# Half of the second layer's weight conversion moved behind the recurrence, as whole tiles in SBUF

## The chip, the cores and the metric

The kernel runs on one core of a Trainium2 chip. The metric is the device time of one execution in microseconds (us); the time of a kernel is the median of several executions. The engines are named as the profile names them: PE (TensorE matmuls), PEld (TensorE weight loads), DVE (VectorE), ACT (ScalarE), POOL (GpSimd) and SP (SyncE, which here issues nearly all DMAs). Each engine works through its own instructions in order, and waits for semaphores.

## The reference

A recurrence over 768 steps for 32 heads (batch 4, 8 heads, width 40) is followed by two feed-forward layers on 3072 tokens. All weights arrive as float64.

```
for t in range(S):                      # recurrence, per head
    y[t]  = r[t] @ state
    Sa    = state @ a[t]
    state = state * w[t] - outer(Sa, b[t]) + outer(v[t], k[t])
x = relu(y @ w_in) ** 2 @ w_out         # layer 0: 320 -> 2048 -> 320
h = x @ w_in2
out = (h * cos(h)) @ w_out2             # layer 1
```

## The kernel before

**The recurrence in chunks.** The 768 steps are cut into 12 chunks of 64, and one call of `period(c)` (line 1013) writes the instructions of one chunk as 42 ticks. At each tick a table `todo` calls generator steps: `decay`, `gt`, `state`, `merge` and their loads and stores. The order in which these Python calls are made is the order in which every engine meets its instructions; nothing is rearranged later. An engine that waits holds up everything behind it.

**The solver.** Each chunk needs a small triangular system solved: `solve` (line 442) issues 62 elementwise operations and a copy (line 454, `L<-T`). From chunk 2 on it runs on POOL, two or three operations per tick from tick 9 to tick 36. When the copy is done, `solve_store` (lines 461, 463) puts the result in DRAM, `load_t` (lines 470, 476) brings it back in another layout for `merge`, and `solve_load` (lines 434 to 439) brings the next system's `T`, `L` and `l21` in, at tick 6 of the next chunk. All these are DMAs of the SP queue. I call the time from one copy's end to the next a cycle: its front lasts until the next solver's first operation, the rest is its solve phase.

**The layers between.** `Mlp.pipeline` (line 772) is a generator over blocks of 512 tokens (6 per layer) and 16 tiles of 128 hidden units. Of one tile it issues 8 matmuls into `h` (line 839), then 8 into `po` (line 795, layer 0) or 12 into `pt` (line 785, layer 1) for the tile two earlier, and gives control back after every second matmul. In layer 0 a tile takes three ACT operations (lines 693 to 695) and one subtraction on POOL (`gl`, line 696). During the recurrence `period` takes about 1.5 such steps per tick; block 5 of layer 0 needs the last chunk, and so starts behind the recurrence, as does all of layer 1.

**The conversion of float64.** There is no float64 on the engines. `Weights` takes each number as two 32-bit words: `clamp` (two ACT operations, lines 167 and 168, and one on DVE), `bits` (two on DVE), `add` (one on POOL, line 179). `pieces` (line 248) does so by quarter tiles of 256, 128, 160 and 160 columns, one piece every 5 steps: at step 0 SP loads the words into `w` (line 183; 2 buffers), at step 4 comes the clamp, then bits and add, and at step 10 the end. For layer 1 (`second`, line 276) the end is a DMA that stores the float32 piece `u` (2 buffers) to the DRAM tensor `w2f` (line 278). So the clamp of piece k+2 must wait until the store of piece k has landed, and the load of piece k+2 until the add of piece k is done. From chunk 2 on, `period` advances the conversion by one step in each tick (line 1093): first the last four tiles of layer 0, then the 16 tiles of layer 1.

**Behind the recurrence.** A range check (`range_sum`; its matmul `pb` is at line 932) is issued, the recurrence's buffers are given up, and a pool `m3` is opened in their place. While the last block of layer 0 runs, `load_w2` (line 670) fetches each converted tile from `w2f` into `wr` (8 buffers), and `split_w2` (line 675) makes the weights' high and low parts of it two steps ahead of their use. A second program, `General`, stands behind a branch that is not taken with these inputs.

## Time and profile before

| what | value |
|---|---|
| median of 3 runs | 1291.02 us (1290.79 to 1295.07) |
| the profiled execution: time | 1293.38 us |
| its span, first to last instruction | 1291.6 us |
| PE busy in the span | 1075.1 us (83%) |
| DVE, ACT, POOL busy | 712.9 (55%), 702.4 (54%), 671.1 us (52%) |
| DMA moved | 121.74 MB, mean 94 GB/s |
| mean granted TensorE clock | 0.897 of full speed |

The stages have different limits. Until about 871 us the recurrence runs, with layer 0 threaded through it; from then on block 5 of layer 0 (to about 943 us) and layer 1 run alone, and PE hardly pauses. Busy shares over the whole span mix the two. In the rows below, a bracket at a row's end gives the time that the engine was idle before the instruction, and what ended that idle time.

### The profile page before, as it was taken

The numbers are of one execution on the slowest core, as the hardware profiler recorded it, in microseconds if no ns is written. First come the engines' busy times: TensorE is split into PE (matmuls) and PEld (weight loads), VectorE is DVE, ScalarE is ACT, GpSimd is POOL, SyncE is SP. The second block draws the span as 40 slices with busy tenths as digits, with TensorE's granted clock in tenths as the row PEclk, the third lists the DMA queues.
The fourth block names the chain that finished last, engine by engine and source line by source line (L and its number), as shares of the span: only waits on it lengthen the run. The fifth ranks groups of instructions, "written<-read, shape, count | busy, mean of one in ns | idle before, by whom it ended". The sixth has DMA issues, their size and how long they took to land.

```text
span 1291.6 us, 27044 instructions
## 1 busy us (share of the span) xinstructions
PE 1075.1 (83%) x10242; PEld 902.2 (70%) x10242; DVE 712.9 (55%) x1450; ACT 702.4 (54%) x1492; POOL 671.1 (52%) x1067
## 2 busy tenths in 40 slices
PE   3245636787879898969797899799999999999997
PEld 3144536666657676757676678578889999999996
DVE  6869765576656665736665546221197343444432
ACT  4133644566566566655656556556556565655554
POOL 4112585685739482838474747423586333333332
PEclk9985555788979898988898889899999999999998
DMA  6473744546373838373745454413031010101000
GB/s 178 83 170 92 174 113 97 115 94 137 71 182 93 171 82 190 93 156 84 159 128 119 113 131 114 88 41 134 19 117 41 5 46 1 46 1 45 1 21 24
DMA packets 281168, 121.74 MB, mean 94 GB/s; under 512 B 231013, under 2 KB 259173, under 8 KB 279885
## 3 DMA queue, kind: packets, MB, share of 16 engines
q1 hardware_dynamic: 279195, 119.24, 38.8%
q8 instruction: 83, 1.36, 0.4%
q10 hardware_dynamic: 1834, 0.69, 0.2%
q14 instruction: 56, 0.46, 0.1%
HBM read 91.31 MB, written 28.57 MB: 93 GB/s over the span
## 4 chain that ended last, share of the span: by engine, by line
PE 50%; POOL 16%; DMA 12%; DVE 10%; SPq 5%; issue 4%; ACT 3%; POOLq 0%; ACTq 0%; DVEq 0%
PE h L839 22%; PE pt L785 13%; PE po L795 7%; DMA cin<-cin 6%; POOL T L451 5%; POOL ttmp L448 4%; POOL gl L696 3%; DMA w2f<-u 2%; POOL u L179 2%; PE px L573 2%; DVE u L142 2%; DVE T L451 1%; DVE ttmp L448 1%; DVE cin L142 1%; PE pu L581 1%
## 5 line engine op out<-in xcount | busy, mean ns | idle before, releaser
L839 PE MATMUL h<-xh,ws 128*128 128x512 f32 x960 | 333.8, 411 | 22.5 <-ACT g L693 22.2
L839 PE MATMUL h<-xl,ws 128*128 128x512 f32 x576 | 235.5, 409 | 0.0
L839 PEld LDWEIGHTS h<-xh,ws 128*128 128x128 f32 x960 | 185.9, 195 | 66.2 <-ACT g L693 26.2
L724 POOL TENSOR_TENSOR gl<-g,gh 128x512 fp32r<-128x512 f32 x96 | 125.2, 1304 | 190.9 <-ACT gh L723 163.6
L179 POOL TENSOR_TENSOR u<-u,w 128x256 int32<-128x256 int32 (+2 forms) x104 | 75.4, 725 | 222.0 <-DVE u L142 142.3
L696 POOL TENSOR_TENSOR gl<-g,gh 128x512 fp32r<-128x512 f32 x96 | 126.7, 1320 | 116.8 <-ACT gh L695 108.9
L142 DVE TENSOR_SCALAR u<-u 128x256 f32<-128x256 f32 (+2 forms) x208 | 72.5, 349 | 172.9 <-ACT u L167 171.2
L795 PE MATMUL po<-gh,ws 128*128 128x512 f32 x480 | 142.8, 422 | 0.3 <-DVE o L142 0.3
L448 POOL TENSOR_TENSOR ttmp<-T,L 128x126 f32<-128x126 f32 (+22 forms) x310 | 124.9, 403 | 34.0 <-DMA L<-Ls 14.0
L451 POOL TENSOR_TENSOR T<-T,ttmp 128x126 f32<-128x126 f32 (+22 forms) x310 | 131.3, 424 | 19.3
L785 PE MATMUL pt<-ws,gh 128*128 128x320 f32 x768 | 128.1, 308 | 0.5 <-DVE g L142 0.4
L839 PEld LDWEIGHTS h<-xl,ws 128*128 128x128 f32 x576 | 112.5, 195 | 20.2
L785 PEld LDWEIGHTS pt<-ws,gh 128*128 128x128 f32 x768 | 119.9, 188 | 8.3 <-DVE g L142 0.6
L142 DVE SCALAR_TENSOR_TENSOR g<-n,h 128x512 f32<-128x512 int32 x96 | 66.0, 687 | 103.3 <-ACT n L704 100.4
L704 ACT ACTIVATE n<-h 128x512 int32<-128x512 f32 x96 | 57.3, 596 | 119.9 <-PE h L839 119.8
L693 ACT ACTIVATE g<-h 128x512 f32<-128x512 f32 x96 | 57.0, 594 | 109.8 <-PE h L839 109.2
L407 PE MATMUL pgt<-at,cin 40*128 40x104 f32 x768 | 72.1, 329 | 52.1 <-DVE at L142 21.4
L795 PEld LDWEIGHTS po<-gh,ws 128*128 128x128 f32 x480 | 94.0, 201 | 24.0 <-issue 1.7
L142 DVE TENSOR_TENSOR g<-g,h 128x512 f32<-128x512 f32 x96 | 65.8, 685 | 71.7 <-ACT g L708 71.7
L167 ACT ACTIVATE u<-w 128x256 f32<-128x256 f32 (+2 forms) x104 | 40.8, 392 | 117.9 <-DMA w2f<-u 73.7
L407 PEld LDWEIGHTS pgt<-at,cin 40*128 40x128 f32 x768 | 62.0, 230 | 59.1 <-issue 24.9
L795 PE MATMUL po<-gl,ws 128*128 128x512 f32 x288 | 85.5, 400 | 0.0
(100 smaller groups left out, 2308.5 us busy)
## 6 DMA issues: line engine op xcount, KB each, us to landing
rv<-rv SPq DMA_DIRECT2D x48, 256.0 KB
cin<-cin SPq DMA_DIRECT2D x11, 832.0 KB
w<-moe SPq DMA_DIRECT2D x12, 704.0 KB
w<-moe SPq DMA_DIRECT2D x40, 160.0 KB
Ls<-ga SPq DMA_DIRECT2D x48, 128.0 KB
L<-Ls SPq DMA_DIRECT2D x48, 128.0 KB
wr<-w2f SPq DMA_DIRECT2D x16, 352.0 KB
w<-moe SPq DMA_DIRECT2D x20, 256.0 KB
```

The costliest lines, as they stand in the source:

```text
L142: fn(*args, **kwargs)
L179: self.nc.gpsimd.tensor_tensor(t.bitcast(I32), u.bitcast(I32), w[:, :, 0], op=ALU.add)
L407: nc.tensor.matmul(pv[par][:, j], self.kb[r0:r0 + 40, p0 + j].rearrange("p h b -> p (h b)"), self.at[r0:r0 + 40, p0 + j], start=True, stop ...
L448: eng.tensor_tensor(tv, T[:, 0:r, j:j + 1].to_broadcast([128, r, n]), L[:, j:j + 1, j + 1:32].to_broadcast([128, r, n]), op=ALU.mult)
L451: eng.tensor_tensor(T[:, 0:r, j + 1:32], T[:, 0:r, j + 1:32], tv, op=ALU.add)
L693: nc.scalar.activation(g, h, AF.Relu)
L696: self.later.append((2, lambda: nc.gpsimd.tensor_tensor(gl, g, gh, op=ALU.subtract)))
L704: nc.scalar.activation(n, h, AF.Copy, bias=0.25, scale=float(np.float32(1.0 / (2.0 * np.pi))))
L724: nc.gpsimd.tensor_tensor(gl, g, gh, op=ALU.subtract)
L785: nc.tensor.matmul(self.pos[j][:, 0:DM], x[:, 128 * j:128 * j + 128], wo[:, DM * ws:DM * ws + DM], start=(f == 0 and x is gh and ws == 0), ...
L795: nc.tensor.matmul(self.pos[m], wo[:, 128 * ws:128 * ws + 128], x, start=(f == 0 and k in (0, 2, 4)), stop=(f == NF - 1 and k in (5, 6, 7)))
L839: nc.tensor.matmul(h, wi[:, ws], x[:, kt], start=(k == 0), stop=(k == 7))
```

## The change

`LATE = 8`: `second` now converts only tiles 0 to 7 of layer 1 in pieces during the recurrence, and from chunk 4 on `period` advances this conversion only at even ticks. Tiles 8 to 15 are converted by a new generator `late`, one step of which follows each step of the layers behind the recurrence: whole tiles of 704 columns, in new staging tiles `w3` (2 buffers), every 14 steps, straight into `wr`, which has 16 buffers now. They are neither written to `w2f` nor read back. `load_w2` fetches tiles 0 to 7 alone. The rest of the diff (arguments `layer` of `split` and `first`, and the weights of `General`) concerns only the branch not taken. The solver is on POOL from chunk 2 on in both kernels.

```diff
+LATE = 8
     def second(self):
-        return self.pieces("moe2", range(NF), 5, lambda f, c0, u: self.nc.sync.dma_start(
+        return self.pieces("moe2", range(LATE), 5, lambda f, c0, u: self.nc.sync.dma_start(
             self.f32[f, :, c0:c0 + u.shape[1]], u))
+
+    def late(self, pool):
+        if not self.raw:
+            return iter(())
+        def job(f):
+            st = {}
+            def load():
+                st["w"] = pool.tile([128, NW, 2], I32, tag="w3", name="w3", bufs=2)
+                self.load("moe2", f, st["w"])
+            def clamp():
+                st["u"] = self.m.raw[f] = pool.tile([128, NW], F32, tag="wr", name="wr", bufs=NF)
+                self.clamp(st["w"], st["u"])
+            return [(0, load), (8, clamp), (12, lambda: self.bits(st["w"], st["u"])),
+                    (17, lambda: self.add(st["w"], st["u"], st["u"]))]
+        return self.stages([job(f) for f in range(LATE, NF)], 14)
...
-            if self.w2 is not None and blk is blocks[-1][1]:
-                self.load_w2(f, self.w2, self.p3, 8)
+            if self.w2 is not None and blk is blocks[-1][1] and f < self.loads:
+                self.load_w2(f, self.w2)
...
-        while self.mlp(64) == 64:
-            pass
+        late = self.W.late(self.M.p3)
+        while self.mlp(1):
+            step(late)
...
-            if c >= 2:
+            if c >= 2 and (c < 4 or t % 2 == 0):
                 step(self.w2, 1)
```

How the order moves, at three places. First SP in the front of the cycle whose copy stands at 687.08 us, from the loads of `tt` to those of `L` (`w<-moe` loads a piece, `w2f<-u` stores one). Before:

```order
L476 DMA tt<-Ts 32x16x32 x4
L183 DMA w<-moe 128x512
L278 DMA w2f<-u 128x160
L421 DMA Ls<-ga 64x8x64
L183 DMA w<-moe 128x256
L278 DMA w2f<-u 128x160
L510 DMA rv<-rv 128x512
L421 DMA Ls<-ga 64x8x64 x2
L510 DMA rv<-rv 128x512
L518 DMA mov<-vt 64x4x40 x2
L434 DMA T<-kti 128x512
L437 DMA L<-Ls 32x32x32 x4
```

Of the two pairs one is left, and it stands later. After:

```order
L500 DMA tt<-Ts 32x16x32 x4
L445 DMA Ls<-ga 64x8x64
L534 DMA rv<-rv 128x512
L185 DMA w<-moe 128x512
L281 DMA w2f<-u 128x160
L445 DMA Ls<-ga 64x8x64 x2
L534 DMA rv<-rv 128x512
L542 DMA mov<-vt 64x4x40 x2
L458 DMA T<-kti 128x512
L461 DMA L<-Ls 32x32x32 x4
```

Second, POOL from the copy at 754.82 us into the next solve. Before:

```order
L454 COPY L<-T 64x512
L179 TENSOR_TENSOR u<-u,w 128x160
L696 TENSOR_TENSOR gl<-g,gh 128x512
L179 TENSOR_TENSOR u<-u,w 128x256
L179 TENSOR_TENSOR u<-u,w 128x128
L696 TENSOR_TENSOR gl<-g,gh 128x512 x2
L448 TENSOR_TENSOR ttmp<-T,L 128x31
L451 TENSOR_TENSOR T<-T,ttmp 128x31
```

Three adds of `u` stood between the copy and the solver's first operation, and one does now. After:

```order
L478 COPY L<-T 64x512
L720 TENSOR_TENSOR gl<-g,gh 128x512
L181 TENSOR_TENSOR u<-u,w 128x160
L720 TENSOR_TENSOR gl<-g,gh 128x512 x2
L472 TENSOR_TENSOR ttmp<-T,L 128x31
L475 TENSOR_TENSOR T<-T,ttmp 128x31
```

Third, SP where the recurrence ends (`xs<-yt` stores the last outputs, `xf<-xs` loads block 5's input, `xf<-x2s` layer 1's first; `wr<-w2f` fetches converted tiles). Before:

```order
L547 DMA xs<-yt 40x8x64 x2
L653 DMA xf<-xs 128x4x128 x2
L653 DMA xf<-xs 64x4x128 x2
L656 DMA xf<-x2s 128x512 x2
L656 DMA xf<-x2s 64x512 x2
L731 DMA x2s<-o 128x512 x2
L731 DMA x2s<-o 64x512
L673 DMA wr<-w2f 128x704 x13
```

The first whole tile's load (`w_9935`, a buffer of `w3`) stands ahead of block 5's input, the second ahead of the block's stores, and the rest among the fetches. After:

```order
L571 DMA xs<-yt 40x8x64 x4
L185 DMA w_9935<-moe 128x1408
L677 DMA xf<-xs 128x4x128 x2
L677 DMA xf<-xs 64x4x128 x2
L680 DMA xf<-x2s 128x512 x2
L680 DMA xf<-x2s 64x512 x2
L185 DMA w_10004<-moe 128x1408
L755 DMA x2s<-o 128x512 x2
L755 DMA x2s<-o 64x512
L185 DMA w_10066<-moe 128x1408
L697 DMA wr<-w2f 128x704 x2
L185 DMA w_10120<-moe 128x1408
```

## Rows read from the trace of the kernel before

**Rows 1.** The page: busy time, share of span, instructions, by engine.
```profile
PE 1075.1 (83%) x10242; PEld 902.2 (70%) x10242; DVE 712.9 (55%) x1450; ACT 702.4 (54%) x1492; POOL 671.1 (52%) x1067
```
**Rows 2.** Busy time by stage: length, PE PEld DVE ACT POOL, clock, DMA share, GB/s.
```profile
349.00:819.00 470.00, 404.73 (x4898) 322.05 (x4894) 278.39 (x598) 278.77 (x651) 293.14 (x557) 0.90 0.57 128
819.00:871.00 52.00, 47.78 (x509) 36.82 (x508) 11.97 (x30) 25.49 (x57) 11.98 (x12) 0.92 0.29 66
871.00:943.00 72.00, 71.97 (x318) 59.38 (x318) 13.23 (x23) 43.04 (x70) 33.70 (x31) 1.00 0.23 78
943.00:1291.60 348.60, 339.48 (x1891) 307.34 (x1890) 165.04 (x241) 191.33 (x322) 148.82 (x132) 0.99 0.09 31
```
**Rows 3.** POOL from 345 to 782 us: copies, and the solver's first operation behind three.
```profile
347.31 1.66 POOL L454 COPY L<-T 64x512 f32<-64x512 f32 x1
...
374.64 0.25 POOL L448 TENSOR_TENSOR ttmp<-T,L 128x31 f32<-128x31 f32 x1
...
418.11 1.39 POOL L454 COPY L<-T 64x512 f32<-64x512 f32 x1
...
440.09 0.24 POOL L448 TENSOR_TENSOR ttmp<-T,L 128x31 f32<-128x31 f32 x1 [0.71 <-DMA L<-Ls]
...
754.82 1.14 POOL L454 COPY L<-T 64x512 f32<-64x512 f32 x1
...
780.66 0.24 POOL L448 TENSOR_TENSOR ttmp<-T,L 128x31 f32<-128x31 f32 x1 [1.70 <-DMA L<-Ls]
...
816.71 1.15 POOL L454 COPY L<-T 64x512 f32<-64x512 f32 x1
```
**Rows 4.** SP in the front behind the copy at 687.08 us: issue times.
```profile
688.28 0.49 SPq L461 DMA_DIRECT2D Tn<-L  x1
...
694.52 0.43 SPq L183 DMA_DIRECT2D w<-moe  x1
695.00 0.43 SPq L278 DMA_DIRECT2D w2f<-u  x1
...
704.81 3.65 SPq L437 DMA_DIRECT2D L<-Ls  x4
```
**Rows 5.** ACT in the same front.
```profile
699.09 0.43 ACT L167 ACTIVATE u<-w 128x256 f32<-128x256 f32 x1 [10.68 <-DMA w2f<-u]
```
**Rows 6.** ACT's waits from 349 to 818 us: total, times, longest.
```profile
ACT u L167 <- DMA w2f<-u: 67.5, 19, 10.7
```
**Rows 7.** ACT's same wait in the cycle from 419 to 481 us alone.
```profile
ACT u L167 <- DMA w2f<-u: 1.3, 1, 1.3
```
**Rows 8.** POOL's groups, 349 to 818 us: busy, mean ns, idle before.
```profile
L451 POOL TENSOR_TENSOR T<-T,ttmp 128x126 f32<-128x126 f32 (+22 forms) x217 | 92.4, 426 | 14.2
...
L179 POOL TENSOR_TENSOR u<-u,w 128x160 int32<-128x160 int32 (+2 forms) x59 | 37.9, 643 | 95.0 <-DVE u L142 41.4 <-ACT ga L427 9.2 <-ACT l L491 8.6
```
**Rows 9.** POOL inside the solve that follows: an add that waits.
```profile
720.08 0.52 POOL L179 TENSOR_TENSOR u<-u,w 128x160 int32<-128x160 int32 x1 [4.84 <-ACT w L168]
```
**Rows 10.** SP, PE and ACT where the recurrence ends.
```profile
866.86 2.59 SPq L653 DMA_DIRECT2D xf<-xs  x4
...
870.59 0.19 PE L932 MATMUL pb<-kc,worst 104*1 104x1 f32 x2
...
872.04 1.85 ACT L667 ACTIVATE xh<-xf 128x512 fp32r<-128x512 f32 x3 [1.06 <-PE h L839]
```
**Rows 11.** ACT: a clamp of 384 columns, and one of 160 that waited for its load.
```profile
188.51 0.55 ACT L167 ACTIVATE u<-w 128x384 f32<-128x384 f32 x1
...
239.37 0.35 ACT L167 ACTIVATE u<-w 128x160 f32<-128x160 f32 x1 [6.82 <-DMA w<-moe]
```
**Rows 12.** Two microseconds of the fetches of `wr` (columns as in rows 2).
```profile
891.00:893.00 2.00, 2.00 (x10) 1.65 (x10) 0.63 (x2) 1.42 (x3) 0.31 (x1) 1.00 1.01 377
```
**Rows 13.** DVE and POOL side by side in layer 1's first block.
```profile
951.47 1.38 POOL L724 TENSOR_TENSOR gl<-g,gh 128x512 fp32r<-128x512 f32 x1 [0.17 <-DMA xf<-x2s]
...
951.61 1.32 DVE L142 TENSOR_SCALAR ws<-wr,kc 128x128 fp32r<-128x128 f32 x1
```

More of the change, by code (lines that the diff above doesn't have):

```diff
@@ L195, in stages, with split @@
             yield
-    def split(self, t, u, c0):
+    def split(self, t, u, c0, layer=0):
         n = u.shape[1]
@@ L206, in split @@
             self.nc.scalar.activation(t[:, q:q + b - a], s, AF.Copy, scale=scale)
-            for lo2, hi2, at2 in (low,) if low else ((640, NW, 640 + DM), (384, 640, 640 + 384)):
+            for lo2, hi2, at2 in (low,) if low else ((384, NW, 640 + DM),) if layer else (
+                    (640, NW, 640 + DM), (384, 640, 640 + 384)):
                 a2, b2 = max(lo2, a), min(hi2, b)
@@ L211, in split, with first @@
                                                  t[:, at + a2 - lo:at + b2 - lo], op=ALU.subtract)
-    def first(self, last=NF):
-        m = self.m
+    def first(self, last=NF, layer=0):
+        m, nm = self.m, ("moe", "moe2")[layer]
         def job(f):
@@ L220, in load @@
             def load():
-                st["dst"] = m.weight_tile(0, f)
+                st["dst"] = m.weight_tile(layer, f)
                 if self.raw:
@@ L224, in load @@
                         I32).rearrange("p a b -> p (a b)")[:, 0:2 * NW].rearrange("p (a b) -> p a b", b=2)
-                    self.load("moe", f, st["w"])
+                    self.load(nm, f, st["w"])
             def begin(c0, n):
@@ L231, in begin @@
                 else:
-                    self.nc.sync.dma_start(u, self.i["moe"][f, :, c0:c0 + n])
+                    self.nc.sync.dma_start(u, self.i[nm][f, :, c0:c0 + n])
             out = [(0, load)]
@@ L239, in job @@
                             (t + 2, lambda c0=c0, n=n: self.add(st["w"][:, c0:c0 + n], st[c0], st[c0]))]
-                out.append((t + 4, lambda c0=c0: self.split(st["dst"], st[c0], c0)))
+                out.append((t + 4, lambda c0=c0: self.split(st["dst"], st[c0], c0, layer)))
             return out
@@ L668, in split_x, with load_w2 @@
             self.vec.tensor_tensor(xl[:, kt], xs[kt], xh[:, kt], op=ALU.subtract)
-    def load_w2(self, f, src, pool, bufs):
-        t = self.raw[f] = pool.tile([128, NW], F32, tag="wr", name="wr", bufs=bufs)
+    def load_w2(self, f, src):
+        t = self.raw[f] = self.p3.tile([128, NW], F32, tag="wr", name="wr", bufs=NF)
         self.nc.sync.dma_start(t, src[f])
@@ L901, in __init__ @@
         self.W = Weights(tc, self.ctx1, i, self.M, self.vec, self.w2f)
-        self.M.w2 = self.w2f
+        self.M.w2, self.M.loads = self.w2f, LATE if self.W.raw else NF
         nb = nch // 2
@@ L1125, in run @@
                 with ExitStack() as cw:
-                    for _ in Weights(tc, cw, g.i, m, g.vec, g.w2f).first():
-                        pass
-                self.layer(m, 0)
-                with ExitStack() as cw:
-                    p = cw.enter_context(tc.tile_pool(name="cw", bufs=2))
-                    for f in range(NF):
-                        m.load_w2(f, g.w2f, p, 2)
-                        m.split_w2(f)
-                self.layer(m, 1)
+                    w = Weights(tc, cw, g.i, m, g.vec, g.w2f)
+                    for layer in range(2):
+                        m.xn = None
+                        for _ in w.first(layer=layer):
+                            pass
+                        self.layer(m, layer)
     def layer(self, m, layer):
```

## The prediction

> **What bounds the kernel now.** I read the page first: PE is busy 83% of the span, no other engine over 55% [rows 1]. The stages then show two limits. From 871 us on PE is busy 71.97 of 72 us and then 339.48 of 348.6 at a clock of 1.00 and 0.99, so that stretch is matmuls alone, and the change takes none away [rows 2]. Between 349 and 819 us, where the recurrence and layer 0 share the engines, PE is busy 404.73 of 470 us and POOL 293.14 [rows 2]: no engine is full, so a chain across engines sets the pace. It repeats with the solver. Its copies end seven cycles between 347.31 and 816.71 us, so a cycle takes 469.4 / 7 = 67.1 us [rows 3]. The front, from the end of a copy to the next solver's first operation, is 374.64 - 348.97 = 25.7 us in the first of the seven, 440.09 - 419.50 = 20.6 in the second and 780.66 - 755.96 = 24.7 in the last [rows 3]; over all seven, measured alike, the mean is 23.6. That leaves 43.4 us to the solve phase.
>
> In the front SP works through stores and loads with few pauses, from the store of the solution at 688.28 to the issue of the four loads of L at 704.81, and the next solver waits for those [rows 4]. In the same front ACT stands still for 10.68 us: it waits for the store of a converted piece, which SP could only issue at 695.00, behind the solver's own stores and loads [rows 4, 5]. With ACT stand everything behind it, layer 0's g and gh, DVE's bits and POOL's gl. In all ACT waits 67.5 us for such stores between 349 and 818 us, 19 times [rows 6], that is 9.6 us per cycle. One cycle shows what it is worth: from 419 to 481 us the wait is only 1.3 us [rows 7], and this cycle has the shortest front, 20.6 us. In the solve phase POOL runs the solver's operations of 0.43 us, and between them the adds of the conversion, 59 of 0.643 us in the seven cycles with their edges [rows 8]. They stand in order, so an add whose clamp came late holds the solver: 4.84 us in one case [rows 9]. Over the seven solve phases I find 27.9 us of such waits (for adds, gl and L together), 4.0 per cycle.
>
> **The change, part by part.**
>
> *Pieces taken out of the recurrence.* 8 tiles of 4 pieces go. By the order, the seven cycles hold 58 adds before and 30 after. Each piece takes with it one load, one store, two operations on ACT, three on DVE, one on POOL. What remains is stepped at half the rate, so between the store of piece k and the clamp of piece k+2 lie 8 ticks instead of 4; at 67.1 / 42 = 1.6 us a tick that is 12.8 us instead of 6.4. In the front that I read the store was issued 6.7 us after the first of the solver's stores and ACT went on 4.1 us later, 10.8 us together [rows 4, 5]. 12.8 is more than that, 6.4 is less, so I expect most of the 67.5 us of ACT waits to go.
>
> *The front.* When the ACT wait goes, what is late next is SP's own queue and the loads of L. I take the front of the cycle that hardly had the wait, 20.6 us, less one pair of load and store that no longer stands ahead of L (0.43 + 0.43 and the gaps, 1.0 us [rows 4]), plus 1.1 us because three of the seven cycles also carry four loads xf of about 2.6 us and this one did not (the like of them at the end takes 2.59 us [rows 10]). That is 20.7 us, 2.9 less than 23.6. Bounds: 0, if another wait of the front is as late, and 9.6, the whole wait.
>
> *The solve phase.* Of some six adds per solve phase three go, 3 x 0.643 = 1.9 us. Of the 4.0 us of waits I credit half, 2.0, since half of the adds remain and gl still waits for ACT. Together 3.9 us; bounds 1.9 and 5.9.
>
> *Per cycle* 2.9 + 3.9 = 6.8 us, which makes it 60.3. The first of the seven fronts still begins with pieces at the old rate, so I count 6.5 cycles: 44 us. PE sets a limit to what can be had: it is idle 470 - 404.73 = 65.3 us in these cycles, 9.3 per cycle [rows 2], which is more than 6.8, but less than the sum of the upper bounds; only where PE's clock of 0.90 rises does its busy time shrink too. In the last chunk the conversion ends earlier and its store pushes ACT less: I take 2 us of the 4.2 that PE is idle from 819 to 871 us [rows 2], bounds 0 and 4.
>
> *The hand-over.* The first whole tile's load stands on SP ahead of block 5's input, and its buffer lies where the recurrence's buffers were, the last of which is read by the matmul pb at 870.59 us [rows 10]. So the loads xf, issued from 866.86 us now, wait for pb, with the whole tile in front of them: about 4.4 us later to be issued (871.3), and 0.72 MB more at 377 GB/s [rows 12] is 1.9 us. ACT took the input at 872.04, having waited only for PE, so it was there by 871 [rows 10]; it would now come near 877, 5 us after ACT takes it today. PE has matmuls of block 4 to go on with for about 1 us more than it needs. So PE loses about 4 us, once; bounds 1 and 6.
>
> *Eight whole tiles beside block 5.* Two ACT operations of 704 columns each: from 0.35 us at 160 and 0.55 at 384 columns [rows 11] I work out 0.35 + 544 x 0.20 / 224 = 0.84 us, so 8 x 2 x 0.84 = 13.4 us. ACT is busy 43.04 of the 72 us of that stretch [rows 2]; with 13.4 more it is at 56.4, so block 5's matmuls cover it. POOL goes from 33.70 us by eight adds of at most 4 x 0.643 (four pieces in one) to at most 54.3 of 72, DVE from 13.23 by some 2 to 3 us a tile. SP's fetches of wr halve. I take 1 us; bounds 0 and 13.4, which is the cost where ACT's cover is gone. Tiles 8 to 15 are wanted only in layer 1's first block, behind all of this.
>
> *Sum.* -44 - 2 + 4 + 1 = -41 us on the profiled execution of 1293.38 us: 1252.4 us. The median of the runs lies 2.4 us lower, so 1250 us.
>
> **The rivals.**
>
> *PE is the bound already.* In the seven cycles PE is the fullest engine by far [rows 2]. If its matmuls had to take the 404.73 us they take now and its pauses came from other causes than the conversion, a cycle would stay at 67 us: 1291 + 5 = 1296 us. Against it speaks that PE's busy time is 57 to 58 us in an average cycle, and that the cycle that hardly had the wait was the one with the shortest front [rows 3, 7]. The Trainium skill (Perfetto Trace Analysis, section Identifying the Most-Contended Engine) says that the engine with the highest occupancy is the one to optimize first; it adds that for TensorE weight-load time is a better measure than matmul time. By the first half nothing is gained here; by the second, with PEld busy 322.05 of 470 us, there is room. Chance 0.06.
>
> *Another wait takes the place.* The state chain, the loads of the next chunk's input and gl behind gh are as late as the stores were, so that the ACT wait goes but the front stays; only the adds in the solve phase count: 6.5 x 1.9 = 12 us, less 5 at the hand-over, 1284 us. For it speaks that POOL also waits for gh and L in the front [rows 3, 8]; that half of the pieces still queue behind the solver's stores, so that the wait may halve and not go, ends in the same place. Chance 0.14.
>
> *Slower: the whole tiles hold up block 5.* A clamp stands on ACT ahead of the g that PE needs. In the recurrence a clamp once waited 6.82 us for its load [rows 11]. The load of tile k+2 can be issued only when tile k has been added, and its clamp comes 19 steps after that add; a step is two matmuls of 71.97 / 318 = 0.226 us [rows 2], so 8.6 us. If landing takes longer than this plus the few us that layer 0's two tiles of lead give, each tile stops PE. At 6.8 us for each of eight tiles that is 54 us, which more than eats the gain: 1304 us. Against it: 0.72 MB at 377 GB/s is 1.9 us, and DMA is busy 23% of that stretch [rows 2, 12]. Chance 0.08. A DVE operation of layer 1's first block took 1.32 us beside a POOL operation of 1.38 [rows 13]; if the three whole-tile DVE operations met gl in the same way, each could delay gl by about its own length. The Trainium skill (SBUF — State Buffer, section Who interferes with whom) says that DVE in its two-port modes and GpSimd hold a shared port pair by turns, for a whole instruction; whole tiles hold it longer than pieces, so the rule speaks against this part of the change. The rows agree that such pairs last alike. It is in the 0.08.
>
> **How the numbers follow.** My forecast, cycles shorter by 4 to 9 us, has 0.72, the rivals 0.06, 0.14 and 0.08. The forecast's own range: 9.3 us per cycle with 4 in the last chunk and 1 at the end gives 1291 - 60 - 4 + 1 = 1228, and a clock nearer to 1.00 some 8 us less; 4 us per cycle with 8 us at the end gives 1291 - 26 + 8 = 1273. The range of 8 in 10 reaches on to the second rival: 1222 to 1283 us. A measurement of this kernel can tell about 0.5% from no change, 6.5 us, so 1284.5 and 1297.5 are the borders. Faster: 0.72 and half of the second rival, 0.79. Within: the other half and part of the first, 0.10. Slower: 0.11, the third rival and what is left of the first.
>
> **What would show it right or wrong.** Right: the seven cycles between the copies at 60 us; ACT's wait of u for w2f from 67.5 to under 20 us; fronts near 21; a pause of PE of some 4 us where block 5 begins, and PE full behind it; from layer 1's first matmul to the end unchanged at 349 us. Wrong: cycles still at 65 us or more with the ACT wait gone (then the second rival), or PE pauses of several us that repeat every 14 steps in block 5 (then the third).

## The result

The changed kernel takes 1270.91 us, the median of 4 runs (1269.0 to 1273.07); the kernel before, run beside it, 1292.4 us (1290.79 to 1295.07, 4 runs). The ratio is 0.983 (95% interval 0.981 to 0.986). The forecast was 1250 us, so the sign and the range held, but of 41 us only 21.5 came.

The profiled execution of after has a span of 1269.3 us, 22.3 less than the span before. Cut in the same stages as [rows 2] it reads as follows (columns: stretch and length; busy time and count of PE, PEld, DVE, ACT and POOL; granted clock; DMA share; GB/s).

```profile
348.00:792.00 444.00, 401.26 (x4914) 320.59 (x4910) 245.59 (x511) 263.27 (x596) 272.55 (x528) 0.92 0.53 117
792.00:846.00 54.00, 51.56 (x522) 40.66 (x521) 9.69 (x21) 23.36 (x49) 12.26 (x11) 0.91 0.22 48
846.00:920.00 74.00, 69.67 (x303) 56.05 (x302) 38.67 (x46) 54.01 (x85) 45.57 (x37) 1.00 0.45 154
920.00:1269.30 349.30, 340.22 (x1896) 307.91 (x1894) 165.38 (x242) 192.04 (x323) 149.54 (x133) 0.99 0.07 23
```

The seven cycles take 444 us instead of 469, and PE is busy nearly as long in them as before (401.26 and 404.73 us). Layer 1 takes 349 us as before. The cycles and their fronts can be read from POOL's row, as in [rows 3]:

```profile
346.35 1.77 POOL L478 COPY L<-T 64x512 f32<-64x512 f32 x1
...
371.84 0.24 POOL L472 TENSOR_TENSOR ttmp<-T,L 128x31 f32<-128x31 f32 x1
...
477.84 1.15 POOL L478 COPY L<-T 64x512 f32<-64x512 f32 x1
...
498.93 1.28 POOL L720 TENSOR_TENSOR gl<-g,gh 128x512 fp32r<-128x512 f32 x1 [16.16 <-ACT gh L719]
503.45 1.28 POOL L720 TENSOR_TENSOR gl<-g,gh 128x512 fp32r<-128x512 f32 x1 [3.25 <-ACT gh L719]
504.70 0.23 POOL L472 TENSOR_TENSOR ttmp<-T,L 128x31 f32<-128x31 f32 x1
...
791.15 1.12 POOL L478 COPY L<-T 64x512 f32<-64x512 f32 x1
```

From the end of the copy at 346.35 to that of the copy at 791.15 are seven cycles, 63.5 us each (before 67.0). The first front ends at 371.84 and takes 23.7 us, the third ends at 504.70 and takes 25.7; the mean of the seven is 22.6 (before 23.6). The solve phase has a mean of 40.8 (before 43.4). The last matmul of the recurrence, `pb`, starts at 842.65 instead of 870.59 us [rows 10]. So the recurrence as a whole gave 27.9 us: 24.7 in the seven cycles, 0.9 ahead of them, 2.3 in the last chunk. From there to layer 1's last matmul `pt` it takes 417.2 us instead of 411.5: 5.7 us given back.

ACT's wait for the stores of pieces, 67.5 us in [rows 6], is nearly gone, as forecast. What is left of it in after, over the seven cycles (columns: engine, line, what it waited for; us in total, times, longest):

```profile
ACT u L169 <- DMA w2f<-u: 7.0, 1, 7.0
```

POOL's waits in the same stretch:

```profile
POOL gl L720 <- ACT gh L719: 90.7, 21, 16.2
POOL u L181 <- DVE u L144: 23.2, 9, 10.1
POOL gl L720 <- PE pu L606: 14.2, 1, 14.2
...
POOL ttmp L472 <- DMA L<-Ls: 4.1, 3, 2.3
```

POOL now stands for `gl` where it stood mostly for the adds (95.0 us in [rows 8]). So the wait that I took for the price of the front went away, and the front hardly moved. That is what the experiments are about.

### The profile page after: what moved, and what is told of

Same layout as the page of the kernel before. It is cut to its first block, busy times and chain, and to the rows that moved or that the text cites. A ratio compares the mean times of both kernels' runs of the same rounds, so it can differ in the third digit from the quotient of the medians.

```text
span 1269.3 us, 26741 instructions
## 1 busy us (share of the span) xinstructions
PE 1071.2 (84%) x10242; PEld 900.0 (71%) x10242; DVE 702.9 (55%) x1378; ACT 696.4 (55%) x1444; POOL 663.2 (52%) x1043
## 4 chain that ended last, share of the span: by engine, by line
PE 48%; POOL 20%; DMA 11%; DVE 10%; issue 5%; SPq 4%; ACT 2%; POOLq 0%; ACTq 0%; DVEq 0%
PE h L863 21%; PE pt L809 13%; POOL T L475 7%; PE po L819 6%; POOL ttmp L472 6%; DMA cin<-cin 6%; POOL gl L720 3%; POOL u L181 2%; DMA xf<-xs 1%; PE px L597 1%; DVE T L475 1%; DVE ttmp L472 1%; DMA t<-Tn 1%; DVE cin L144 1%; PE pu L605 1%
## 5 line engine op out<-in xcount | busy, mean ns | idle before, releaser
L863 PEld LDWEIGHTS h<-xh,ws 128*128 128x128 f32 x960 | 184.9, 194 | 62.6 <-ACT g L717 20.1
L475 POOL TENSOR_TENSOR T<-T,ttmp 128x126 f32<-128x126 f32 (+22 forms) x310 | 128.7, 415 | 20.1
L181 POOL TENSOR_TENSOR u<-u,w 128x384 int32<-128x384 int32 (+2 forms) x72 | 54.7, 760 | 136.9 <-DVE u L144 108.9
L819 PEld LDWEIGHTS po<-gh,ws 128*128 128x128 f32 x480 | 94.0, 202 | 25.9 <-ACT o L767 1.9
L144 DVE TENSOR_SCALAR u<-u 128x160 f32<-128x160 f32 (+9 forms) x144 | 50.5, 351 | 99.7 <-ACT u L169 88.9
L144 DVE TENSOR_TENSOR mov<-pu,kc 64x416 f32<-64x416 f32 x96 | 56.5, 588 | 83.8 <-PE pu L606 81.4
```

The source lines that it names most:

```text
L144: fn(*args, **kwargs)
L181: self.nc.gpsimd.tensor_tensor(t.bitcast(I32), u.bitcast(I32), w[:, :, 0], op=ALU.add)
L475: eng.tensor_tensor(T[:, 0:r, j + 1:32], T[:, 0:r, j + 1:32], tv, op=ALU.add)
L819: nc.tensor.matmul(self.pos[m], wo[:, 128 * ws:128 * ws + 128], x, start=(f == 0 and k in (0, 2, 4)), stop=(f == NF - 1 and k in (5, 6, 7)))
L863: nc.tensor.matmul(h, wi[:, ws], x[:, kt], start=(k == 0), stop=(k == 7))
```

## The experiments

Four questions: what ends the front, what sets the solve phase, what the end costs, and whether a version is better than both. In the tables, "L issued" is the time from a copy's end until SP has issued the next solver's loads of L and l21. All columns but the ratio are means of seven cycles of one profiled execution (`pb` to `pt`: one stretch, from the start of `pb` to the start of the last row of `pt`), worked out from the rows of POOL, SP and PE. Each ratio is to the kernel before on the same chip.

| kernel | ratio (interval) | cycle | front | L issued | solve | `pb` to last `pt` |
|---|---|---|---|---|---|---|
| before | 1 | 67.0 | 23.6 | 21.7 | 43.4 | 411.5 |
| after | 0.983 (0.981 to 0.986) | 63.5 | 22.6 | 20.7 | 40.8 | 417.2 |
| u4 | 0.999 (0.997 to 1.001) | 67.5 | 23.4 | 21.9 | 44.1 | 411.5 |
| no_add | 0.987 (0.984 to 0.989) | 64.5 | 24.0 | 21.8 | 40.5 | 411.5 |
| no_pieces | 0.964 (0.961 to 0.967) | 61.4 | 21.5 | 19.7 | 39.8 | 416.1 |
| full_rate | 0.985 (0.981 to 0.988) | 64.6 | 23.0 | 20.7 | 41.6 | |
| front_empty | 1.002 (1.000 to 1.003) | 67.9 | 22.6 | 21.1 | 45.4 | |
| sp_clear | 0.996 (0.994 to 0.998) | 66.6 | 20.8 | 19.5 | 45.8 | |
| thin_pe | 0.976 (0.974 to 0.978) | 63.0 | 22.1 | | 40.9 | |
| no_late | 0.978 (0.976 to 0.980) | 63.5 | 22.3 | | 41.2 | 411.6 |
| x_first | 0.981 (0.978 to 0.983) | 64.0 | 22.5 | | 41.5 | 414.9 |
| late12 | 0.982 (0.979 to 0.984) | 61.8 | 22.0 | 19.6 | 39.8 | 428.9 |
| l12p12 | 0.982 (0.979 to 0.985) | 61.7 | 22.0 | 19.9 | 39.8 | 425.5 |
| best | 0.995 (0.993 to 0.997) | 64.4 | 20.1 | 18.7 | 44.4 | |

**Is ACT's wait for the store worth anything?** u4 is the kernel before with four buffers `u` instead of two, so that a clamp need not wait for the store two pieces back.

```diff
-PIECES = ((0, 256), (256, 128), (384, 160), (544, 160))
+PIECES = ((0, 176), (176, 176), (352, 176), (528, 176))
-                st["u"] = self.p.tile([128, 256], F32, tag="u", name="u", bufs=2)[:, 0:n]
+                st["u"] = self.p.tile([128, 176], F32, tag="u", name="u", bufs=4)[:, 0:n]
```

> The kernel before, with four buffers for the converted piece u instead of two, and pieces of 176 columns four times instead of 256, 128, 160 and 160 so that they fit. All adds stay on POOL; only the wait of a clamp for an earlier store can go. If that wait set the cycles (the prediction's front term), ACT's wait of u for w2f falls from 67.5 us to under 10, the seven cycles from 67.1 to about 64, and the time to about 1270 us. If the adds on POOL were what counted (rival: another wait takes the place), the wait goes and the cycles stay at 66 to 67: 1285 to 1292 us.

Measured: no gain (0.999), fronts of 23.4 us. Of the wait for the store 4.0 us are left, but ACT's waits show another in its place, at the same instruction:

```profile
ACT u L167 <- DMA w<-moe: 62.7, 19, 8.8
```

It is as long and as frequent as the one before: 62.7 us, 19 times, now for the load of the piece, whose buffer POOL's add sets free. So this run does not show what a front without any wait of ACT would be; that the wait for the store alone is worth nothing, it shows.

**What do the pieces cost in all?** no_pieces is the changed kernel with the pieces of tiles 1 to 7 left out (layer 1 takes tile 0's copy for them); full_rate is the changed kernel with a step of the conversion in each tick, so that its pieces end halfway through the seven cycles.

```diff
-        return self.pieces("moe2", range(LATE), 5, lambda f, c0, u: self.nc.sync.dma_start(
+        return self.pieces("moe2", range(1), 5, lambda f, c0, u: self.nc.sync.dma_start(
-        self.nc.sync.dma_start(t, src[f])
+        self.nc.sync.dma_start(t, src[0])
```

And full_rate:

```diff
-            if c >= 2 and (c < 4 or t % 2 == 0):
+            if c >= 2:
```

> The changed kernel without the conversion of tiles 1 to 7 of layer 1: tile 0 alone is converted in pieces, and its stored copy is fetched for all of tiles 0 to 7, so that from chunk 4 on no conversion runs beside the recurrence. Tiles 8 to 15 as in the changed kernel. It measures what the conversion that is left costs, and what the cycles are without any. If SP's queue and the loads of L bound the front, the last pair of load and store leaving it gives fronts of about 20 us instead of 22.6; if PE with the merge chain and gl bounds it, the fronts stay at 22 to 23. The solve phases lose three adds (1.9 us) and their waits: 40.8 to about 38. Cycles 60 to 61 us, time 1245 to 1253 us.

> The changed kernel with the conversion stepped at every tick again: the pieces of tiles 0 to 7 are done by chunk 8, and later chunks have none. If the wait for the stores sets the cycles, the cycles of chunks 4 to 7 are like those before (67 us, ACT waiting for w2f as before) and the last ones near 60 us; in sum 1265 to 1275 us. If the half rate is what helped and not the number of pieces, the first cycles are worse than the last by over 6 us. If neither matters much in the front, all cycles differ by the adds alone (2.6 us).

Measured: without pieces the cycle falls to 61.4 us, the front to 21.5 (between the two cases of the expectation) and the solve phase to 39.8, less far than expected. This is about the floor for taking pieces away (only the first front still has some), and it settles one thing against my sum: taking out *all* pieces shortens the front by 2.1 us and the solve phase by 3.5, while I had booked 2.9 and 3.9 for taking out *half* of them. full_rate takes as long as the changed kernel: its first four cycles with pieces are 70.1, 65.6, 70.4 and 64.7 us long, the last three without 62.6, 59.3 and 59.5. The first are worse by 7.2 us on average, yet the total is that of the changed kernel. So it matters how many pieces lie in the seven cycles, and hardly how they are spread.

**Which part of a piece costs?** no_add is the kernel before without POOL's add in the pieces of the second layer; loads, stores and the operations on ACT and DVE stay.

```diff
-                    (6, lambda: self.add(st["w"], st["u"], st["u"])), (period + 5, lambda: end(f, c0, st["u"]))]
+                    (6, lambda: nm == "moe2" or self.add(st["w"], st["u"], st["u"])),
+                    (period + 5, lambda: end(f, c0, st["u"]))]
```

> The kernel before with one operation left out: GpSimd's add of the low word in the pieces of the second layer's weights (all 32 tiles' loads, stores, clamps and DVE operations stay; the converted weights lack the low word). 58 adds of 0.643 us fall out of the seven cycles, 37 us of POOL, and with them the waits that they pass on. Theory one (a piece costs what its add costs in POOL's order): the gain of the change, which took out 28 of the 58, is passed by far; about 0.8 us for each of the 58 adds, 45 us, so 1247 us, cycles at 61 us, at the least 25 us of gain. Theory two (what counts is the rest of a piece: its load and store on SP and its operations on ACT and DVE): all of that stays, so 1285 to 1297 us and cycles at 66 to 67 us. In between, near 1270 us: both in equal parts.

Measured: 0.987, near the case that I had called "both in equal parts". The two halves lie apart: the solve phase falls by 2.8 us, the front not at all (24.0). Without any piece the front falls too (no_pieces). So the adds cost in the solve phase, and something else of a piece in the front; that it is the loads and stores, the runs on the front show below. Even with no add left the solve phase is at 40.5, since POOL now waits for something else. Its longest wait over the seven cycles is at layer 0's `gl`:

```profile
POOL gl L697 <- ACT gh L696: 153.1, 29, 20.1
```

Most of it lies in the fronts; 4.1 us per cycle of waits at `gl` lie in the solve phases, where before had 0.6.

**What ends the front?** Either POOL's `gl`, which stands in POOL's order ahead of the solver and waits up to 16 us, or the loads of L. front_empty keeps layer 0's steps out of the front (first diff). sp_clear (second) brings the loads `xf` behind L on SP. It was to bring the pieces' loads and stores there too, but its rows still show one pair ahead of L in six of the seven fronts, as in the changed kernel. Since the block's start moves with `xf`, layer 0's late `gl` leave the four fronts concerned as well.

```diff
-                self.acc += RATE
+                self.acc += RATE if c < 4 or c > 10 else RATE * 42 / 28 if 9 <= t < 37 else 0.0
```
```diff
-            if c >= 2 and (c < 4 or t % 2 == 0):
+            if c >= 2 and (c < 4 or t > 9 and t % 3):
-            if c % 2 == 0 and c and t == 2:
+            if c % 2 == 0 and c and t == (2 if c == 2 else 10):
-            if c % 2 == 0 and t == (FIRST - 3 if c == 2 else 5):
+            if c % 2 == 0 and t == (FIRST - 3 if c == 2 else 13):
```

> The changed kernel with layer 0's steps moved out of the fronts: in chunks 4 to 10 they are issued only in ticks 9 to 36, at 1.5 times the rate; all work stays. Theory one (the front, 22.6 us in the changed kernel, ends late because POOL's gl stands in it ahead of the solver and waits for PE and ACT, up to 16 us at a time): fronts fall below 20 us; if the solve phase (40.8 us) takes the moved work without growing by as much, cycles go to 61 us and the time to 1253 us. Theory two (SP's stores and the loads of L end the front anyway): fronts stay at 21.5 to 23 us and solve phases grow, so 1271 us or more. Theory three (PE has no room left for a cycle this short): fronts shorten and solve phases grow by the same, cycles at 63 to 64 us, 1266 to 1276 us.

> The changed kernel with SP's queue cleared ahead of the solver's loads of L: the four loads xf (2.6 us, in three of the seven cycles) and the loads and stores of the pieces come behind L instead of ahead of it; all work stays. Theory one (the front ends when SP has worked through its issues: L and l have been issued 21.7 us after a copy's end in the kernel before and 20.7 us in the changed one, and the solver starts 1.9 us later in both): 1.0 us of pieces and 3/7 of 2.6 us fall out, so L is issued by 18.6 us, fronts go from 22.6 to 20.5 us, and the time to 0.97 of the kernel before, 1255 us against 1292. Theory two (POOL's gl, which waits for PE and ACT, ends the front): fronts stay at 22 to 23 us and the time between 0.98 and 0.985 of before. A price there may be: block inputs that come later keep PE waiting for xh or xl in the solve phase.

Measured: with at most one `gl` in a front, right behind the copy, the front is 22.6 us, exactly as in the changed kernel; POOL then waits for L in its place, in all seven. POOL in one such front:

```profile
490.99 1.12 POOL L478 COPY L<-T 64x512 f32<-64x512 f32 x1
496.18 0.79 POOL L181 TENSOR_TENSOR u<-u,w 128x160 int32<-128x160 int32 x1 [4.07 <-DVE u L144]
515.90 0.24 POOL L472 TENSOR_TENSOR ttmp<-T,L 128x31 f32<-128x31 f32 x1 [18.93 <-DMA L<-Ls]
```

SP in the same front:

```profile
492.14 0.49 SPq L485 DMA_DIRECT2D Tn<-L  x1
492.68 1.37 SPq L487 DMA_DIRECT2D Ts<-T  x2
...
499.24 0.57 SPq L185 DMA_DIRECT2D w<-moe  x1
499.85 2.18 SPq L281 DMA_DIRECT2D w2f<-u  x1
502.13 0.38 SPq L534 DMA_DIRECT2D rv<-rv  x1
502.55 2.61 SPq L677 DMA_DIRECT2D xf<-xs  x4
...
510.35 3.19 SPq L461 DMA_DIRECT2D L<-Ls  x4
513.63 1.13 SPq L463 DMA_DIRECT2D l<-Ls  x2
```

From 492.14 to 514.76 SP issues one DMA behind the other, and the solver starts 1.1 us later. So theory two holds: SP's row ends the front where `gl` is out of the way. sp_clear shortens that row (L is issued 1.2 us sooner), and the front follows by 1.8 us, to 20.8. The four fronts that lost the loads `xf` show it best, since no late `gl` stands in them in either run: they have a mean of 23.5 us in front_empty and 20.4 in sp_clear, and the four issues `xf` took 2.6 us. The counts agree: ahead of L stand two pairs of load and store in before's fronts (three in one), one in after (two in the first), none in no_pieces (two in the first), and L is issued after 21.7, 20.7 and 19.7 us. A pair is 1.0 us, and the front is 1.9 us longer than that time in all three. In the changed kernel SP's row is not alone, though: POOL's view above has three waits for L, so three fronts of seven end with L, and the other four end right behind a `gl` that waited for `gh`, as the third does. Both rows end close to each other, and taking away one gives little while the other stands. The Trainium skill (Perfetto Trace Analysis, section What "DMA-bound" means) names the issuing engine's own row, solid with DMA issues, as one of the things that bind; this case agrees, for the front only.

Neither kernel gained, though. In sp_clear the four cycles that carry `xf` have solve phases of 51.1, 49.1, 48.7 and 42.9 us, because the block's input now comes late where its operations are due. PE's longest wait over the seven cycles:

```profile
PE h L863 <- ACT g L717: 41.0, 4, 11.6
```

And ACT's, over the same stretch:

```profile
ACT xh L691 <- DMA xf<-xs: 43.1, 9, 11.4
```

ACT stands for `xf` up to 11.4 us at a time, PE for ACT behind it. That is the price which the expectation had named, and it was larger than the gain. In front_empty the solve phase grows by 4.5 us: two to three more `gl` (7 or 8 instead of 5) are 3.0 us of POOL, and its waits at `gl` grow from 0.8 to 4.2 us, while the solver and the waits of the adds give some back.

**What sets the solve phase?** PE is busy 41.21 of 41.50 us in one solve phase of after, POOL only 35.50. That front and solve phase by the view of stretches (columns as above):

```profile
479.00:504.70 25.70, 19.67 (x284) 15.54 (x283) 12.68 (x25) 15.91 (x34) 4.64 (x5) 0.80 0.83 171
504.70:546.20 41.50, 41.21 (x474) 33.02 (x473) 28.79 (x60) 26.55 (x62) 35.50 (x73) 1.00 0.38 94
```

I took PE for the limit there. thin_pe is the changed kernel with two of the eight matmuls `h` of layer 0 left out while the recurrence runs.

```diff
                 for k, (ws, x, kt) in enumerate(seq):
-                    nc.tensor.matmul(h, wi[:, ws], x[:, kt], start=(k == 0), stop=(k == 7))
+                    if self.p3 is not None or k not in (1, 4):
+                        nc.tensor.matmul(h, wi[:, ws], x[:, kt], start=(k == 0), stop=(k == 7))
```

> The changed kernel with less for PE to do and all else alike: while the recurrence runs, layer 0's first product leaves out two of its eight matmuls (two of the three that take xl, the low part of the input). In the seven cycles that is about 113 of 452 matmuls h, which take 132 us there, so 33 us of PE or 4.7 per cycle, about 3.8 of it in a solve phase. Theory one (in the solve phase PE is the bound: busy 41.2 of 41.5 us in one of the changed kernel's and 36.3 of 36.3 in another): solve phases fall from 40.8 to 38.3 us or less, fronts stay at 22.6, and the time is 0.968 of the kernel before or less. Theory two (POOL's row of solver operations, adds and gl sets the solve phase, PE only fills the time): solve phases stay within 1 us of 40.8 and the time at 0.978 to 0.985. If the fronts shorten too, PE has a part in them.

Measured: theory one falls. Solve phases stay at 40.9 us on average, with PE idle 4.5 us in them where it was 2.6. The third and the fourth of them:

```profile
500.70:539.80 39.10, 34.35 (x391) 27.35 (x386) 25.54 (x52) 23.68 (x54) 34.65 (x71) 0.96 0.42 100
560.20:602.90 42.70, 33.21 (x386) 26.58 (x381) 21.14 (x46) 20.84 (x49) 32.61 (x71) 0.88 0.37 93
```

PE has room in both, though its clock was lower than in the row of after (0.96 and 0.88), and the cycle is only 0.4 us shorter. Single phases vary: the third fell from 41.5 to 39.1 us, as theory one has it, and the fourth rose from 40.0 to 42.7, so only the mean tells. The ratio of 0.976 is below after's and just below what I had said for theory two (0.978 to 0.985), but only 3.0 of the 8.5 us between the spans come from the seven cycles, 1.9 from ahead of them and 2.8 from the last chunk. With PE out, POOL's row is left, on which the solve phase begins and ends. Its parts, in us per solve phase (waits without the one of the first operation, which ends the front; "rest" is the small gaps between operations):

| kernel | solver | adds | gl | waits of adds | waits of gl | rest | sum |
|---|---|---|---|---|---|---|---|
| before | 26.6 | 3.2 | 6.6 | 3.0 | 0.6 | 3.4 | 43.4 |
| after | 26.2 | 1.7 | 6.6 | 1.7 | 0.8 | 3.8 | 40.8 |
| thin_pe | 26.1 | 1.8 | 6.5 | 2.2 | 0.5 | 3.8 | 40.9 |
| no_add | 25.7 | 0 | 6.6 | 0 | 4.1 | 4.1 | 40.5 |
| no_pieces | 25.9 | 0.1 | 6.4 | 0.3 | 2.9 | 4.1 | 39.8 |

Two-thirds of it is the solver itself, and of after's 40.8 us POOL waits for others in only 2.5. Where the adds go, their waits go, but `gl` is then reached earlier and waits for `gh`: 4.1 us in no_add, 2.9 in no_pieces.

**What does the end cost?** no_late is the changed kernel without the conversion of tiles 8 to 15 (layer 1 takes the copies of tiles 0 to 7 for them); x_first starts that conversion three steps of layer 0 later, so that the loads `xf` stand ahead of the first whole tile.

```diff
-            step(late)
+            pass
```
```diff
         self.ready = nch
         late = self.W.late(self.M.p3)
+        self.mlp(3)
```

> The changed kernel without its new second part: tiles 8 to 15 aren't converted when the recurrence has ended; in their place layer 1 fetches the stored copies of tiles 0 to 7 again (so the weights of eight tiles are other ones). Sixteen fetches as in the kernel before. If the whole tiles, with their loads ahead of block 5's input, cost the 5.7 us by which the time from pb to layer 1's first matmul has grown (72.8 to 78.5 us), this goes back to 73 us and the time to 1265 us. If the pause at the hand-over comes from the recurrence's end itself, it stays at 78 us and the time at 1271 us. The cycles before it must stay at 63.5 us in either case.

> The changed kernel with the late conversion begun two steps of the layers later, so that on SP the loads of block 5's input stand ahead of the first whole tile's load. If the hand-over cost is the late input (my term of 4 us), the pause of PE of 2 us and the waits behind it go, the time from the range check's matmul to layer 1 falls from 78.5 to about 75 us, and the kernel takes about 1267 us. If the loss is in the eight whole tiles beside block 5 instead, it stays at 1271 us.

Measured: in no_late the stretch from `pb` to the last `pt` is 411.6 us, as in the kernel before, in u4 and in no_add (411.5). The time is 0.978 (0.976 to 0.980) of before; the interval just misses the changed kernel's, and 0.5% of 1299 is 6.5 us. So the whole 5.7 us come from the late conversion. x_first gets 2.3 of them back (414.9); its total can't be told from after's, since the intervals overlap, and in the profiled execution, the longest of its five, the cycles were 0.5 us longer. The hand-over in the changed kernel answers to [rows 10]. SP:

```profile
842.91 0.36 SPq L185 DMA_DIRECT2D w<-moe  x1
843.33 2.58 SPq L677 DMA_DIRECT2D xf<-xs  x4
```

ACT, with the first whole tile's clamp (two operations) behind the input, then the first operation of the second's, and `o`, the output of the block before:

```profile
848.32 0.63 ACT L691 ACTIVATE xh<-xf 128x512 fp32r<-128x512 f32 x1 [5.28 <-DMA xf<-xs]
...
852.41 0.82 ACT L169 ACTIVATE wr<-w 128x704 f32<-128x704 f32 x1
853.13 0.84 ACT L170 ACTIVATE w<-w 128x704 int32<-128x704 uint32 x1
...
858.62 0.84 ACT L169 ACTIVATE wr<-w 128x704 f32<-128x704 f32 x1 [0.78 <-DMA w<-moe]
...
860.10 1.06 ACT L767 ACTIVATE o<-po 128x512 f32<-128x512 f32 x2
```

PE, every wait of over 0.3 us up to 864:

```profile
849.00 0.50 PE L863 MATMUL h<-xh,ws 128*128 128x512 f32 x1 [1.99 <-ACT xh L691]
...
860.73 1.22 PE L819 MATMUL po<-gh,ws 128*128 128x512 f32 x4 [1.29 <-ACT o L767]
862.55 0.50 PE L819 MATMUL po<-gh,ws 128*128 128x512 f32 x1 [0.60 <-DVE o L144]
```

As forecast, the whole tile waits for `pb` (842.65) and the input stands behind it; PE then loses 2.0 us for `xh` and 1.9 for `o`, which stands on ACT behind the second whole tile's clamp. In x_first the wait for `o` is gone, and one of 1.6 us for `xh` is left.

**Is there a better version?** late12 has twelve whole tiles, one every 9 steps, and half as many pieces; l12p12 the same number every 12 steps, with the pieces early; best has sp_clear's order of the loads `xf` on top of that. All three start as x_first does.

```diff
-LATE = 8
+LATE = 4
-        return self.stages([job(f) for f in range(LATE, NF)], 14)
+        return self.stages([job(f) for f in range(LATE, NF)], 9)
-            if c >= 2 and (c < 4 or t % 2 == 0):
+            if c >= 2 and (c < 4 or t % 4 == 0):
```
```diff
-        return self.stages([job(f) for f in range(LATE, NF)], 14)
+        return self.stages([job(f) for f in range(LATE, NF)], 12)
-            if c >= 2 and (c < 4 or t % 2 == 0):
+            if c >= 2:
```

> Twelve tiles converted as whole tiles behind the recurrence where the changed kernel has eight, in place of every second piece that is left (15 adds of pieces in the seven cycles where the changed kernel has 30), a whole tile every 9 steps, and block 5's input ahead of the first of them. If each piece that leaves the recurrence is worth 0.8 us, 12 us less there, and four more whole tiles cost 1 to 3 us at the end: 1259 to 1262 us. If the tail has no room for twelve tiles, block 5 shows pauses that come back every 9 steps and the time is 1271 us or more.

> Twelve whole tiles once more, now one every 12 steps instead of 9, and the 16 pieces that are left stepped in every tick, so that they end near the first of the seven cycles. In the run with a tile every 9 steps, ACT waited 1.3 to 2.7 us for the load of each whole tile and PE then 1.2 to 1.4 us for ACT, four times, and from pb to layer 1's last matmul pt it took 428.9 us where the changed kernel took 417.2. If these waits come from the short period, the tail returns to 415 to 418 us, and with cycles at 61 us the time is 0.97 of the kernel before (1254 us against 1292). If they come from the number of tiles, the tail stays at 425 us or more and the time is 0.978 or more.

> Both together: twelve whole tiles, one every 12 steps, the pieces early, and the loads xf behind the solver's loads of L. If SP's issues end the front and the tail holds, cycles come to 59 to 60 us, and the time to 0.96 to 0.965 of the kernel before (1243 us against 1292). If only one of the two holds, 0.97.

Measured: none is told from the changed kernel by its time, except best, which is slower. In late12 the seven cycles gave 11.3 us, close to the 12 expected, and the end took 11.7 us back: 428.9 us from `pb` to the last `pt`. Its ACT in block 5 shows how:

```profile
872.48 0.84 ACT L169 ACTIVATE wr<-w 128x704 f32<-128x704 f32 x1 [1.84 <-DMA w<-moe]
873.23 0.83 ACT L170 ACTIVATE w<-w 128x704 int32<-128x704 uint32 x1
873.95 0.58 ACT L717 ACTIVATE g<-h 128x512 f32<-128x512 f32 x1
...
877.81 0.85 ACT L169 ACTIVATE wr<-w 128x704 f32<-128x704 f32 x1 [1.95 <-DMA w<-moe]
```

And three of PE's pauses in the same place:

```profile
874.58 0.50 PE L863 MATMUL h<-xh,ws 128*128 128x512 f32 x1 [1.26 <-ACT g L717]
879.93 0.50 PE L863 MATMUL h<-xh,ws 128*128 128x512 f32 x1 [1.40 <-ACT g L717]
885.01 0.50 PE L863 MATMUL h<-xh,ws 128*128 128x512 f32 x1 [1.15 <-ACT g L717]
```

A clamp waits for its tile's load, `g` behind it comes late, and PE stops: my third rival, which the eight tiles of the changed kernel set off only once (the 0.78 us before a clamp, above), and twelve at this pace do again and again. With a tile every 12 steps these pauses are gone, and others stand there, where layer 1's input is split (PE's waits from `pb` to the first `pt`):

```profile
PE h L863 <- DVE xl L144: 4.1, 2, 3.9
PE h L863 <- ACT xh L691: 3.3, 2, 1.7
```

So the end is 425.5 us: it is the number of tiles more than their pace. What in these later pauses holds up DVE and ACT was not taken apart. best shows again that the front does follow SP (20.1 us) and that the late input costs more than that (solve phases 44.4).

## Why the prediction was right, and where it was too large

**Right in kind.** Layer 1 at 349 us, the wait for the stores from 67.5 to 7.0 us, whole-tile operations of 0.82 and 0.84 us where I worked out 0.84, PE nearly full from block 5 on: these came as said. The last chunk was priced at 2 and gave 2.3. The end was priced at 4 + 1 = 5 us and measured at 5.7, in part by luck: PE idles 4.6 us in the 22 us behind `pb`, but of these only some 2.5 are the late input, priced at 4, and 1.9 are the wait for `o`, which falls to the whole tiles, priced at 1. The forecast itself, cycles shorter by 4 to 9 us, just missed: they are 3.5 us shorter, neither near 60 us nor at 65. The time lies within the forecast's own bound of 1273 us all the same, because the end did not cost the 8 us that this bound allowed, and because the last chunk and the stretch ahead of the cycles gave 3.2 us that it left out.

**The front, -2.9 per cycle, was the step that failed.** It measured -1.0. I read ACT's wait as what held the front, because the cycle that hardly had it [rows 7] had the shortest front [rows 3]. That cycle was short for another reason that stands on SP's row: it has no loads `xf`, and its L was issued 18.8 us after the copy, against 21.7 on average. The trace of before could have told. ACT's same wait in its fourth, fifth and seventh front alone:

```profile
ACT u L167 <- DMA w2f<-u: 10.4, 1, 10.4
ACT u L167 <- DMA w2f<-u: 1.7, 1, 1.7
ACT u L167 <- DMA w2f<-u: 0.5, 1, 0.5
```

These fronts last 22.1, 23.7 and 24.7 us: the one with the long wait is the shortest of the three, and the two that hardly have it carry `xf`. In the front that I took for my example ACT's wait did reach SP, by way of DVE's operations behind it. SP's waits there have this line:

```profile
SPq L421 <- DVE u L142: 2.3, 1, 2.3
```

That front, the sixth, went from 23.4 to 20.3 us. I took one front of seven for all. The text had the right cause in it: "what is late next is SP's own queue and the loads of L", with 1.0 us for one pair of load and store. This pair is about all that came on average. Four of the seven cycles carry the loads `xf`, not three, which alone makes the front that I worked out 0.4 us too short. Over 6.5 cycles I had booked 18.9 us here, and 7.1 came.

**The solve phase, -3.9 per cycle, was the second term mis-sized.** It measured -2.5. A solve phase holds 5.1 adds in before and 2.7 in after, so 2.4 go and not three; they gave 1.5 us of the 1.9 booked. Of the waits I credited 2.0 and 1.0 came (3.5 to 2.5; my 4.0 had counted in the waits for L, which end the front). The solver's own operations gave 0.4, and the small gaps took 0.4 back. The runs no_add and no_pieces show why half of the waits was too much to ask: a wait for an add that goes is in part replaced by one for `gh`. Booked 25.4 us, measured 17.6.

**The rivals.** Rival two, another wait in its place, describes the front, and half of the waits in the solve phase; with its 1284 us it went too far, since the front's pair of DMAs and the last chunk counted as well. Rival one, PE as the bound, took the fullest engine for the limit. PE is at 99% in one solve phase, and yet a quarter fewer matmuls `h` moved the cycle by 0.4 us only. The rule of the Trainium skill cited there (Perfetto Trace Analysis, section Identifying the Most-Contended Engine) would by its first half have PE optimized first, and that run speaks against it. By its caveat, weight loads instead of matmuls, PE is at 33.02 of 41.50 us and POOL at 35.50 is the fullest, which agrees with what the runs show. Rival three occurred with eight tiles only once and in small, and with twelve at 9 steps again and again. Whether DVE's whole-tile operations and `gl` delay each other through a shared port, no run here took apart.

My measure for "what can be had" was also at fault. I allowed PE's idle 9.3 us per cycle as room for 6.8 us of gain. By the stages, 5.7 of them lay in the front, where SP's row sets the end, and only 3.7 in the solve phase, less than the 3.9 that I booked there.

## What to carry to other kernels

Where an engine that issues DMAs runs with hardly a pause up to the transfer that everybody waits for, count the issues that stand ahead of it: here each pair of load and store that left gave 1.0 us per cycle, and a wait of 67.5 us on another engine beside it gave next to nothing on average. One front, or one cycle, is not enough to read a price from: put the wait and the length of all of them side by side. Before a wait is booked as gain, ask what the same instruction, or the next one in its engine's row, waits for when it is gone; where an engine's row is the limit, add up its operations and credit these, and be sparing with the waits between them: here 1.0 us of 3.5 went. A busy share of 99% does not make an engine the limit of a stretch: it may be filling time that another engine's row sets.

## What was not expected of the hardware

An engine's issue of DMAs alone took the better part of a front: from a copy to the last load of l21 it took SP 21.7 us in before and 20.7 in after, on average, for some thirty issues, most of 0.4 to 0.7 us each, with short gaps between them. The DMA engines were busy to a share of 0.83 in one such front, the third of after. A whole tile's load together with block 5's input took from 842.91 to 848.32 us to be used, 5.4 us, where 1.9 us were worked out from the rate of other fetches for the tile alone. And PE's granted clock had a mean of 0.80 in the front from 479.00 to 504.70, in which PE was busy 19.67 of 25.70 us, so it stood at the lower of its two levels, 1.2 GHz, in a part of it; in the solve phase behind it PE was busy 41.21 of 41.50 us and the clock was 1.00, 2.4 GHz, throughout.
